# Attention start: tile 0's scores spread in three portions from two queues, tile 1's scores computed before the first head mix

## The chip, the cores and the metric

The kernel runs on one core of a Trainium2 chip. The metric is the device time of one execution in microseconds (us). Of the kernel before there are three runs: 768.92, 771.27 and 774.01 us (median 771.27). One further execution was profiled, and every row below is from it. PE is the matrix engine, DVE the vector engine, ACT the scalar engine, POOL the GpSimd engine, and SP the engine whose queue issues most DMAs.

## What is computed

Attention whose heads are mixed twice, and then two gated or squared feed-forward layers, all in float32. The part that matters is the start of the attention:

```python
scores = scale * np.matmul(q, k.transpose(0, 1, 3, 2))        # 2 batches, 12 heads, 448 x 448
scores = np.einsum('bhij,hg->bgij', scores, w_pre)            # mix of the heads
scores = scores - np.max(scores, axis=-1, keepdims=True)
attn = np.exp(scores)
attn = attn / (np.sum(attn, axis=-1, keepdims=True) + 1e-09)
attn = np.einsum('bhij,hg->bgij', attn, w_post)               # second mix
return np.matmul(attn, v)
```

The feed-forward layers follow: `x = (x @ w_a) * (x @ w_b) @ w_out`, then `relu(x @ w_in) ** 2 @ w_out`.

## The kernel before

The 448 query rows of a batch are cut into four tiles (120, 120, 120 and 88 rows), so that there are eight tiles over the two batches. A tile goes through these steps:

- `load_q` (L119) fetches the tile's queries, `load_k` (L124) one pair of heads' keys.
- `qk(b, t, c)` (L133) computes the scores of heads 2c and 2c+1: two matmuls into two PSUM banks, queries on the partitions. The trace records a float32 matmul as two rows, so one `qk` is "x4".
- `qk_out` (L145) copies each head's scores from PSUM to SBUF (even heads on ACT at L153, odd heads on DVE at L151) and issues the DMA that spreads them into the buffer `G[t % 2]` (L157). After it, partition 13 k + h of G holds head h of ten query rows, and G's second index r counts twelve such groups of ten rows. One DMA per head moves all twelve groups, 210 KB; head 11 needs a second small one of one partition (L160), so a tile has 13 of them, all on SP's queue.
- `premix` (L167) is the first mix: one matmul per group r, which reads G[:, r, :] of all heads. Two groups make a pair m; tile 0 has the pairs 0 to 5. One `premix` call is two matmuls ("x4"). Its PSUM tag T has three banks.
- `smin`, `sexp`, `weights2` (softmax), `post` (L209, second mix), `evac` (L231), `av` (L247) follow pair by pair.

The order on each engine is the order in which the code is written. The main loop runs over the pairs n: `premix` of pair n+1, `qk_out` of what is pending, `post` of pair n, the softmax of pair n+1, then the work that a table `mid` sets for slot n. For the tile after tile 0 the table places `qk` c at slot (c * 3) // 6, so the slots 0, 1 and 2 hold two `qk` each for tile 1. The slots 3 to 8 hold one `qk` each for tile 2. `load_q` of tile 2 stands at slot 0.

Ahead of the loop: SP loads six `ks` (keys) and then the queries of tile 1; POOL's queue loads tile 0's queries, `wpre_sb` and `wp`, and then POOL clears G[0] while DVE clears G[1] (L274, L275). PE runs nine dummy matmuls (`busy(9)`, L282), tile 0's six `qk`, and eighteen dummy matmuls (`busy(18)`). SP issues tile 0's 13 spreads, then the load of `v` (1344 KB) and the queries of tile 2.

Of the kernel before, what the change touches and what calls it, by code (L numbers as in the profile page):

```python
# [7 lines left out]
F32 = mybir.dt.float32  # L8
# [7 lines left out]
B, H, S, D = 2, 12, 448, 64  # L16
# [31 lines left out]
def half_rows(t, r):  # L48
    return KG if (r + 1) * ROW <= ROWS[t] else (ROWS[t] - r * ROW) // 2
# [3 lines left out]
def place(k, h):  # L53
    return 64 if (k, h) == (ROW - 1, H - 1) else PK * k + h
# [3 lines left out]
def attention_moe_kernel(  # L58
# [10 lines left out]
    nc = tc.nc  # L69
# [7 lines left out]
    def ps(tag):  # L77
        return psum.tile([128, 512], F32, tag=tag, name=tag, bufs=PB[tag])
# [5 lines left out]
    wpre_sb = const.tile([128, 128], F32, name="wpre_sb")  # L84
# [5 lines left out]
    def xpair(b, i, dtype):  # L90
        return outer.tile([128, 2, S], dtype, tag=f"x{b}_{i}", name=f"x{b}_{i}")
# [9 lines left out]
    s_p = att.enter_context(tc.tile_pool(name="s", bufs=4))  # L101
    e_p = att.enter_context(tc.tile_pool(name="e", bufs=2))
    a_p = att.enter_context(tc.tile_pool(name="a", bufs=2))

    G = [sb.tile([128, H, S], F32, name=f"G{i}") for i in range(2)]
    A = {}
# [6 lines left out]
    Sps = []  # L113
# [2 lines left out]
    vv = {}  # L116
    AVp = {}

    def load_q(b, t, eng=nc.sync):  # L119
        x = w_p.tile([128, UW], F32, tag="wc", name="q", bufs=2)  # L120
        eng.dma_start(out=x[:, 0:6 * TILE], in_=qT[b, t])
        qq[b, t] = x

    def load_k(b, c, eng=nc.sync):  # L124
        kk[b, c] = single(f"ks{6 * b + c}", F32)
        eng.dma_start(out=kk[b, c], in_=kT[b, c])

    def load_v(b, eng=nc.sync):
        x = sb.tile([JP, NJ, DM], F32, tag="v", name="v")
        eng.dma_start(out=x, in_=v[b])  # L130
        vv[b] = x


    def qk(b, t, c, tags=("qk", "qk")):
        n = ROWS[t]
        p = [ps(tag) for tag in tags]
        for e in range(2):
            o = 64 * e
            nc.tensor.matmul(  # L139
                p[e][0:n, 0:S], qq[b, t][o:o + 64, c * TILE:c * TILE + n], kk[b, c][o:o + 64, :], start=True, stop=True  # L140
            )
        for e in range(2):
            Sps.append((b, t, 2 * c + e, p[e]))

    def qk_out(stage=None):  # L145
        while Sps:
            b, t, h, p = Sps.pop(0)
            n = ROWS[t]
            s = stage[h // 2][0:TILE, h % 2, :] if stage else s_p.tile([TILE, S], F32, tag="s", name="s")
            if h % 2:  # L150
                nc.vector.tensor_copy(s[0:n], p[0:n, 0:S])  # L151
            else:
                nc.scalar.copy(s[0:n], p[0:n, 0:S])  # L153
            g = G[t % 2]
            full = n // ROW
            last = ROW - 1 if h == H - 1 else ROW
            nc.sync.dma_start(out=g[h:PK * (last - 1) + h + 1:PK, 0:full, :], in_=s[0:last * full])  # L157
            if last < ROW:
                o = place(last, h)
                nc.sync.dma_start(out=g[o:o + 1, 0:full, :], in_=s[last * full:ROW * full])  # L160
            rem = (n - full * ROW) // 2
            for f in range(2 if rem else 0):
                o = full * ROW + f * rem
                a = place(f * KG, h)
                nc.sync.dma_start(out=g[a:a + PK * (rem - 1) + 1:PK, full, :], in_=s[o:o + rem])

    def premix(b, m):  # L167
        t, r, n = PAIRS[m]
# [56 lines left out]
    def evac(b, m, f):  # L225
        t, r, n = PAIRS[m]
        if r == 0 and f == 0:
            A[b, t] = a_p.tile([JP, NJ * H, TILE], F32, tag="a", name="a")
        a = A[b, t]
        p = Pps[b, m][f]  # L230
        k = half_rows(t, r + n - 1)  # L231
        src = p[0:JP, 0:n * NJ * H * KG].rearrange("p (n g k) -> p n g k", n=n, k=KG)[:, :, :, 0:k]
        o = r * ROW + f * k
        dst = a[:, :, o:o + (n - 1) * ROW + k]
        if n == 2:
            dst = a[:, :, r * ROW:(r + 2) * ROW].rearrange("p g (n i) -> p n g i", n=2)[:, :, :, f * KG:f * KG + KG]
        else:
            src = src[:, 0]
        if f:
            nc.vector.tensor_copy(dst, src)  # L240
        else:
            nc.scalar.copy(dst, src)
# [23 lines left out]

    warm = const.tile([128, 1], F16, name="warm")
    nc.vector.memset(warm, 0.0)
    load_q(0, 0, nc.gpsimd)
    for c in range(NC):  # L270
        load_k(0, c)
    nc.gpsimd.dma_start(out=wpre_sb, in_=wpre)
    nc.gpsimd.dma_start(out=wp, in_=wpost)
    nc.gpsimd.memset(G[0], 0.0)  # L274
    nc.vector.memset(G[1], 0.0)  # L275
    nc.vector.tensor_scalar(wpre_sb, wpre_sb, -0.125, None, ALU.mult)


    def busy(n):
        p = ps("av")  # L280
        for _ in range(n):
            nc.tensor.matmul(p[0:1, 0:S], warm, warm.to_broadcast([128, S]), start=True, stop=True)  # L282

    busy(9)
    load_q(0, 1)
    stage0 = [xpair(b, i, F32) for b in range(B) for i in range(NC // 2)]
    tags0 = (("qk", "qk"), ("T", "T"), ("post", "post"))
    for c in range(NC):
        qk(0, 0, c, tags0[c % 3])
# [10 lines left out]
    act_l, dve_l, mid = {}, {}, {}  # L300

    def at(d, slot, *f):
        d.setdefault(max(slot, 0), []).append(f)

    for ti, (b, t) in enumerate(tiles):
        s0, sp = base[ti], span[ti]
        if ti + 1 < len(tiles):
            nxt = tiles[ti + 1]
            for c in range(NC):
                at(mid, s0 - 3 + c if ti else (c * (sp - 3)) // NC, qk, *nxt, c)  # L310
            if ti + 2 < len(tiles):
                at(mid, s0 - 2, load_q, *tiles[ti + 2])
            if nxt[1] == NTL - 1 and nxt[0] + 1 < B:
                for c in range(NC):
                    at(mid, s0 + c // 2, load_k, nxt[0] + 1, c)
        if ti > 0:
            pb, pt = tiles[ti - 1]
            for c in range(NC):
                s = s0 + 1 + (c * (sp - 1)) // NC
                at(mid, s, av, pb, pt, c)  # L320
                if c % 2:
                    at(mid, s, av_out, pb, pt, c // 2)
            if pt == NTL - 1 and pb + 1 < B:
                at(mid, s0 + sp, load_v, pb + 1)
# [80 lines left out]
    s0 = base[-1]  # L405
    s1 = base[-2]
# [189 lines left out]
def _layout(i):  # L596
    import numpy as np

    f = np.float32
    q, k, v = i["q"], i["k"], i["v"]  # L600
    qT = np.zeros((B, NTL, 128, NC, TILE), f)
    for t in range(NTL):
        n = ROWS[t]
        full = n // ROW
        p = np.arange(full * ROW)
        col = np.concatenate([ROW * (p % full) + p // full, np.arange(full * ROW, n)]) + OFFS[t]
        x = q[:, :, col, :].reshape(B, NC, 2, n, D).transpose(0, 2, 4, 1, 3)
        qT[:, t, :, :, 0:n] = x.reshape(B, 128, NC, n)
    kT = k.reshape(B, NC, 2, S, D).transpose(0, 1, 2, 4, 3).reshape(B, NC, 128, S)
    vl = v.reshape(B, H, NJ, JP, D).transpose(0, 3, 2, 1, 4).reshape(B, JP, NJ, DM)  # L610
    wpre = np.zeros((128, 128), f)
    wpost = np.zeros((128, H, KG), f)
    for n in range(ROW):
        o = [place(n, h) for h in range(H)]
        wpre[np.ix_(o, o)] = i["w_pre"]
        wpost[o, :, n % KG] = i["w_post"]

    def units(m):
        kk, n = m.shape
        x = m.reshape(kk // 128, 128, n // 128, 128).transpose(2, 0, 1, 3)  # L620
        return x.reshape(-1, US, 128, 128).transpose(0, 2, 1, 3).reshape(-1, 128, US * 128)

    ua, ub = units(i["moe_w_a"]), units(i["moe_w_b"])
    ab = np.stack([ua, ub], 1).reshape(-1, 128, US * 128)
    wall = np.concatenate([ab, units(i["moe_w_out"]), units(i["moe2_w_in"]), units(i["moe2_w_out"])], 0).view(np.uint64)
    return {"qT": qT.reshape(B, NTL, 128, NC * TILE), "kT": kT, "v": vl, "wpre": wpre, "wpost": wpost, "w": wall}
# [20 lines left out]
```

## Time and profile before

| what | value |
|---|---|
| runs | 768.92, 771.27, 774.01 us |
| the profiled execution | 769.89 us |
| its span (first to last instruction) | 768.1 us |
| PE busy | 745.7 us, 97% of the span |
| DVE, ACT, POOL busy | 63%, 40%, 2% |
| SP's queue and the like (hardware queue), share of 16 DMA engines | 33.2% |

The span is 1.8 us shorter than the execution's own time. The chain of waits that ended last is PE for 95% of the span. The page cuts the span into 40 slices of 19.2 us: PE's row begins 6, 7 and is 8 or 9 in tenths from the third slice on, and PE's granted clock is 9, 7 and then 9 in tenths.

### The profile page before, as it was taken

The numbers are of one execution on the slowest core, as the hardware profiler recorded it, in microseconds if no ns is written. First come the engines' busy times: TensorE is split into PE (matmuls) and PEld (weight loads), VectorE is DVE, ScalarE is ACT, GpSimd is POOL, SyncE is SP. The second block draws the span as 40 slices with busy tenths as digits, with TensorE's granted clock in tenths as the row PEclk, the third lists the DMA queues.
The fourth block names the chain that finished last, engine by engine and source line by source line (L and its number), as shares of the span: only waits on it lengthen the run. The fifth ranks groups of instructions, "written<-read, shape, count | busy, mean of one in ns | idle before, by whom it ended". The sixth has DMA issues, their size and how long they took to land.

```text
span 768.1 us, 12411 instructions
## 1 busy us (share of the span) xinstructions
PE 745.7 (97%) x5055; PEld 617.8 (80%) x5055; DVE 487.4 (63%) x817; ACT 309.1 (40%) x559; POOL 18.0 (2%) x16
## 2 busy tenths in 40 slices
PE   6799999998999999999999999999999999999998
PEld 2356666665667799999999999999999999999997
DVE  4366656565667767676667666556888888654540
ACT  2355554454456443334333323223555554322220
POOL 3000000000002300000000000000000000000000
PEclk9799999999999999999999999999999999999999
DMA  6543243426141113323323323323233332434310
GB/s 215 170 132 102 82 129 116 120 74 188 57 146 58 61 65 125 123 83 123 124 83 124 123 83 124 124 82 124 83 123 101 106 124 88 160 129 134 126 48 36
DMA packets 26696, 84.85 MB, mean 110 GB/s; under 512 B 2896, under 2 KB 16736, under 8 KB 26416
## 3 DMA queue, kind: packets, MB, share of 16 engines
q1 hardware_dynamic: 26496, 83.59, 33.2%
q8 instruction: 40, 0.66, 0.4%
q0 software_dynamic: 144, 0.47, 0.2%
q14 instruction: 16, 0.13, 0.0%
HBM read 62.03 MB, written 2.75 MB: 84 GB/s over the span
## 4 chain that ended last, share of the span: by engine, by line
PE 95%; DMA 2%; SPq 1%; DVE 1%; ACT 0%; issue 0%; ACTq 0%; POOLq 0%
PE T L171 10%; PE post L219 10%; PE T L448 8%; PE T L449 8%; PE T L450 8%; PE qk L448 5%; PE post L449 5%; PE post L448 5%; PE post L450 5%; PE qk L449 5%; PE qk L450 5%; PE av L254 5%; PE qk L139 5%; PE av L450 3%; PE av L449 3%; PE av L448 3%
## 5 line engine op out<-in xcount | busy, mean ns | idle before, releaser
L372 ACT CAST wh<-wc 128x768 fp32r<-128x768 f32 x68 | 56.8, 835 | 122.3 <-DVE wc L366 108.8
L219 PEld LDWEIGHTS post<-w,e 64*112 64x112 f32 x1440 | 74.4, 174 | 29.8 <-PE T L171 21.5
L377 DVE TENSOR_TENSOR wl<-wc,wh 128x768 fp32r<-128x768 f32 x66 | 63.0, 955 | 48.1 <-ACT wh L372 48.1
L187 ACT ACTIVATE e<-T,nb 128x448 f32<-128x448 f32 x90 | 56.9, 633 | 88.0 <-DVE nb L179 87.9
L171 PE MATMUL T<-G,wpre_sb 128*128 128x448 f32 x180 | 82.3, 581 | 8.4 <-DMA G<-x 8.4
L449 PE MATMUL T<-m,wh 128*128 128x448 f32 x237 | 86.6, 365 | 0.0
L448 PE MATMUL T<-m,wh 128*128 128x448 f32 x237 | 86.6, 365 | 0.0
L450 PE MATMUL T<-m,wl 128*128 128x448 f32 x237 | 86.5, 365 | 0.0
L219 PE MATMUL post<-w,e 64*112 64x60 f32 x1440 | 80.5, 261 | 0.1
L179 DVE TENSOR_REDUCE nb<-T 128x1 f32<-128x448 f32 x90 | 55.8, 623 | 28.3 <-PE T L171 23.4
L171 PEld LDWEIGHTS T<-G,wpre_sb 128*128 128x128 f32 x180 | 31.6, 195 | 47.4 <-issue 46.1
L355 DVE SCALAR_TENSOR_TENSOR wa<-wr,wa 128x768 uint32<-128x768 uint32 x68 | 65.2, 959 | 2.3
L366 DVE SCALAR_TENSOR_TENSOR wc<-wc,wa 128x768 uint32<-128x768 uint32 x68 | 65.2, 958 | 2.3
L240 DVE COPY a<-post 112x480 f32<-112x480 f32 (+1 forms) x46 | 30.9, 671 | 49.6 <-PE post L219 49.6
L350 ACT ACTIVATE wc<-wr 128x768 f32<-128x768 f32 x68 | 61.4, 903 | 0.0
L254 PE MATMUL av<-a,v 112*64 112x120 f32 (+1 forms) x768 | 45.2, 264 | 5.2 <-DMA v<-v 3.0
L254 PEld LDWEIGHTS av<-a,v 112*64 112x64 f32 x768 | 37.0, 136 | 15.7 <-PE post L219 4.0
L362 DVE TENSOR_SCALAR wc<-wc 128x768 f32<-128x768 f32 x68 | 38.7, 569 | 16.3 <-ACT wc L350 16.3
L139 PE MATMUL qk<-ks,q 64*120 64x448 f32 (+1 forms) x176 | 44.9, 568 | 4.1 <-DMA q<-qT 2.3
L448 PEld LDWEIGHTS T<-m,wh 128*128 128x128 f32 x237 | 44.5, 188 | 3.5
L449 PEld LDWEIGHTS T<-m,wh 128*128 128x128 f32 x237 | 44.5, 188 | 3.5
L450 PEld LDWEIGHTS T<-m,wl 128*128 128x128 f32 x237 | 44.5, 188 | 3.5
(146 smaller groups left out, 1353.2 us busy)
## 6 DMA issues: line engine op xcount, KB each, us to landing
wr<-w SPq DMA_DIRECT2D x68, 768.0 KB
G<-s SPq DMA_DIRECT2D x55, 210.0 KB
G<-s SPq DMA_DIRECT2D x22, 140.0 KB
ks<-kT SPq DMA_DIRECT2D x12, 224.0 KB
v<-v SPq DMA_DIRECT2D x2, 1344.0 KB
outT<-ta SPq DMA_DIRECT2D x12, 224.0 KB
q<-qT SPq DMA_DIRECT2D x7, 360.0 KB
G<-x SPq DMA_DIRECT2D x11, 210.0 KB
```

The source lines that it names most:

```text
L139: nc.tensor.matmul(p[e][0:n, 0:S], qq[b, t][o:o + 64, c * TILE:c * TILE + n], kk[b, c][o:o + 64, :], start=True, stop=True)
L171: nc.tensor.matmul(p[0:GP, 0:S], wpre_sb[0:GP, 0:GP], G[t % 2][0:GP, r + i, :], start=True, stop=True)
L187: nc.scalar.activation(out=e[0:GP], in_=Tps.pop((b, m, i))[0:GP, 0:S], func=ACTF.Exp, bias=NB[b, m][0:GP, i:i + 1], scale=-1.0, accum_out= ...
L219: nc.tensor.matmul(p[f][0:JP, c:c + k], e[o:o + 64, j * JP:(j + 1) * JP], w2[o:o + 64, i, :], start=True, stop=True,)
L254: nc.tensor.matmul(p[64 * e:64 * e + 64, o:o + n], vv[b][:, j, g * D:(g + 1) * D], A[b, t][:, j * H + g, 0:n], start=(j == 0), stop=(j == ...
L350: nc.scalar.activation(out=st["c"], in_=rd(st["high"]), func=ACTF.Abs, scale=HSC)
L355: nc.vector.scalar_tensor_tensor(out=a, in0=st["high"], scalar=0x80000000, in1=a, op0=ALU.bitwise_and, op1=ALU.bitwise_or)
L366: nc.vector.scalar_tensor_tensor(out=cu, in0=cu, scalar=3, in1=st["a"], op0=ALU.logical_shift_left, op1=ALU.bitwise_or)
L377: eng.tensor_tensor(out=lo, in0=st["c"], in1=rd(st["hi"]), op=ALU.subtract)
L448: nc.tensor.matmul(p[:, 0:S], hi[:, sl], x[0], start=first, stop=False)
L449: nc.tensor.matmul(p[:, 0:S], hi[:, sl], x[1], start=False, stop=False)
L450: nc.tensor.matmul(p[:, 0:S], lo[:, sl], x[0], start=False, stop=last)
```

## The change

Tile 0's scores are spread in three portions of groups: 0 to 1, 2 to 5 and 6 to 11 (`GS`). The first portion's DMAs go out as each head is copied, even heads from SP, odd heads from POOL; the second and third portions are issued by SP, head by head, after that. Groups 0 to 1 are pair 0, groups 2 to 5 the pairs 1 and 2, groups 6 to 11 the pairs 3 to 5. The queries' rows are laid out on the host so that each portion's rows lie together. Tile 1's six `qk` move ahead of the loop, into a staging tile `s1` that takes one of the two buffers of pool `a`, and its 13 spreads are issued by POOL, after POOL has cleared G[1]. Tile 0's queries are loaded in three pieces from ACT's queue, ahead of ACT's table load, and `wpre_sb` behind them. G[0] is cleared in three pieces, by POOL, DVE and POOL. Eighteen dummy matmuls become four.

```diff
+GS = (0, 2, 6, 12)
...
-    def load_q(b, t, eng=nc.sync):
+    def load_q(b, t, engs=(nc.sync,)):
         x = w_p.tile([128, UW], F32, tag="wc", name="q", bufs=2)
-        eng.dma_start(out=x[:, 0:6 * TILE], in_=qT[b, t])
+        n = NC * TILE // len(engs)
+        for i, eng in enumerate(engs):
+            eng.dma_start(out=x[:, i * n:(i + 1) * n], in_=qT[b, t, :, i * n:(i + 1) * n])
         qq[b, t] = x
...
+    def qk_copy(t, h, p, s):
+        n = ROWS[t]
+        if h % 2:
+            nc.vector.tensor_copy(s[0:n], p[0:n, 0:S])
+        else:
+            nc.scalar.copy(s[0:n], p[0:n, 0:S])
+
+
+    def spread(t, h, s, r0, r1, eng=nc.sync):
+        g = G[t % 2]
+        n = r1 - r0
+        o = r0 * ROW
+        last = ROW - 1 if h == H - 1 else ROW
+        eng.dma_start(out=g[h:PK * (last - 1) + h + 1:PK, r0:r1, :], in_=s[o:o + last * n])
+        if last < ROW:
+            a = place(last, h)
+            eng.dma_start(out=g[a:a + 1, r0:r1, :], in_=s[o + last * n:o + ROW * n])
...
-            A[b, t] = a_p.tile([JP, NJ * H, TILE], F32, tag="a", name="a")
+            A[b, t] = a_p.tile([128, NJ * H, TILE], F32, tag="a", name="a")[0:JP]
...
-    load_q(0, 0, nc.gpsimd)
-    for c in range(NC):
+    for c in range(2):
         load_k(0, c)
-    nc.gpsimd.dma_start(out=wpre_sb, in_=wpre)
+    load_q(0, 0, (nc.scalar, nc.scalar, nc.scalar))
+    for c in range(2, NC):
+        load_k(0, c)
+    nc.scalar.dma_start(out=wpre_sb, in_=wpre)
     nc.gpsimd.dma_start(out=wp, in_=wpost)
-    nc.gpsimd.memset(G[0], 0.0)
-    nc.vector.memset(G[1], 0.0)
+    for i in range(3):
+        (nc.gpsimd, nc.vector)[i % 2].memset(G[0][:, GS[i]:GS[i + 1], :], 0.0)
     nc.vector.tensor_scalar(wpre_sb, wpre_sb, -0.125, None, ALU.mult)
...
     for c in range(NC):
         qk(0, 0, c, tags0[c % 3])
-        qk_out(stage0)
+        while Sps:
+            _, t, h, p = Sps.pop(0)
+            qk_copy(t, h, p, stage0[h])
+            spread(0, h, stage0[h], GS[0], GS[1], (nc.sync, nc.gpsimd)[h % 2])
+    nc.gpsimd.memset(G[1], 0.0)
+    for i in range(1, 3):
+        for h in range(H):
+            spread(0, h, stage0[h], GS[i], GS[i + 1])
+    s1 = a_p.tile([128, NJ * H, TILE], F32, tag="a", name="s1").rearrange("p g i -> p (g i)")
+    stage1 = [s1[0:TILE, h * S:(h + 1) * S] for h in range(H)]
+    for c in range(NC):
+        qk(0, 1, c, tags0[c % 3])
+        while Sps:
+            _, t, h, p = Sps.pop(0)
+            qk_copy(t, h, p, stage1[h])
+    for h in range(H):
+        spread(1, h, stage1[h], 0, ROWS[1] // ROW, nc.gpsimd)
     load_v(0)
-    busy(18)
+    busy(4)
...
-            for c in range(NC):
-                at(mid, s0 - 3 + c if ti else (c * (sp - 3)) // NC, qk, *nxt, c)
+            for c in range(NC if ti else 0):
+                at(mid, s0 - 3 + c, qk, *nxt, c)
```

On SP's queue the spreads of tile 0 read so before; each row is one DMA (or "x2" two alike), `x` is the staged scores of tile 0 by pairs of heads, G_83 is G[0].

```order
L157 DMA G_83<-x_0_118 10x12x448 x2
L157 DMA G_83<-x_1_119 10x12x448 x2
L157 DMA G_83<-x_2_120 10x12x448 x2
L157 DMA G_83<-x_0_121 10x12x448 x2
L157 DMA G_83<-x_1_122 10x12x448 x2
L157 DMA G_83<-x_2_123 10x12x448
L157 DMA G_83<-x_2_123 9x12x448
L160 DMA G_83<-x_2_123 1x12x448
L130 DMA v<-v 112x3072
L121 DMA q<-qT 128x720
```

Now the second portion ends and the third one runs as follows; six spreads of two groups and ten more of four stand ahead of these rows.

```order
L162 DMA G_83<-x_2_126 10x4x448
L162 DMA G_83<-x_2_126 9x4x448
L165 DMA G_83<-x_2_126 1x4x448
L162 DMA G_83<-x_0_121 10x6x448 x2
L162 DMA G_83<-x_1_122 10x6x448 x2
L162 DMA G_83<-x_2_123 10x6x448 x2
L162 DMA G_83<-x_0_124 10x6x448 x2
L162 DMA G_83<-x_1_125 10x6x448 x2
L162 DMA G_83<-x_2_126 10x6x448
L162 DMA G_83<-x_2_126 9x6x448
L165 DMA G_83<-x_2_126 1x6x448
L134 DMA v<-v 112x3072
```

Thirteen spreads have become 6 of two groups, 13 of four and 13 of six, 32 in all, and `v` and tile 2's queries stand behind all of them.

On PE the loop's first slots read so before; T is the first mix, post the second.

```order
L171 MATMUL T<-G_83,wpre_sb 128x448 x4
L219 MATMUL post<-w_206,e 112x60 x16
L139 MATMUL qk<-ks_89,q 120x448 x2
L139 MATMUL qk<-ks_91,q 120x448 x2
L171 MATMUL T<-G_83,wpre_sb 128x448 x2
L219 MATMUL post<-w_243,e 112x60 x16
L139 MATMUL qk<-ks_93,q 120x448 x2
L139 MATMUL qk<-ks_95,q 120x448 x2
```

Now the same slots, up to pair 5's first mix in the last row (the T rows are pairs 0 and 1, then 2, 3, 4 and 5):

```order
L185 MATMUL T<-G_83,wpre_sb 128x448 x4
L233 MATMUL post<-w_272,e 112x60 x16
L185 MATMUL T<-G_83,wpre_sb 128x448 x2
L233 MATMUL post<-w_309,e 112x60 x16
L185 MATMUL T<-G_83,wpre_sb 128x448 x2
L233 MATMUL post<-w_347,e 112x60 x16
L185 MATMUL T<-G_83,wpre_sb 128x448 x2
L233 MATMUL post<-w_383,e 112x60 x16
L143 MATMUL qk<-ks_87,q 120x448 x2
L185 MATMUL T<-G_83,wpre_sb 128x448 x2
```

The six `qk` of tile 1 have left the slots 0 to 2; tile 2's first `qk` stays ahead of pair 5.

POOL's queue held three loads and one clear at the start before. Now it reads as follows, from its second clear on (G_84 is G[1], s_203 the staging tile of tile 1):

```order
L291 MEMSET G_83 128x2688
L162 DMA G_83<-x_0_121 10x2x448
L162 DMA G_83<-x_1_122 10x2x448
L162 DMA G_83<-x_2_123 10x2x448
L162 DMA G_83<-x_0_124 10x2x448
L162 DMA G_83<-x_1_125 10x2x448
L162 DMA G_83<-x_2_126 9x2x448
L165 DMA G_83<-x_2_126 1x2x448
L311 MEMSET G_84 128x5376
L162 DMA G_84<-s_203 10x12x448 x11
L162 DMA G_84<-s_203 9x12x448
L165 DMA G_84<-s_203 1x12x448
```

The odd heads' part of the first portion, the clear of G[1] and the 13 spreads of tile 1 stand behind each other on it.

## Rows read from the trace of the kernel before

**Rows 1.** Chain of waits: start us, us, what; the stretch 12 to 30 us
```profile
12.90 0.76 SPq L157
...
16.32 1.10 SPq L157
...
19.20 3.83 DMA G<-x
23.03 0.41 issue
23.44 5.89 PE T L171 x8
```

**Rows 2.** Chain of waits, the loop's first slots
```profile
31.05 0.85 PE qk L139 x4
...
32.47 1.50 PE qk L139 x4
...
40.31 1.70 PE T L171 x4
...
50.87 1.70 PE T L171 x4
52.57 1.71 PE post L219 x32
54.28 0.81 PE qk L139 x4
55.09 1.70 PE T L171 x4
```

**Rows 3.** Timeline of SP's queue: start us, us, line, out<-in, xcount
```profile
8.39 10.75 SPq L157 DMA_DIRECT2D G<-x  x12
...
20.02 1.05 SPq L130 DMA_DIRECT2D v<-v  x1
...
80.62 0.77 SPq L157 DMA_DIRECT2D G<-s  x1
81.48 1.31 SPq L165 DMA_DIRECT2D G<-s  x2
```

**Rows 4.** Timeline of all engines, the first 8 us: [idle before <-releaser]
```profile
0.93 3.52 PE L282 MATMUL av<-warm 128*1 128x448 f16 x9 [0.93 <-DVE warm L268]
1.25 0.69 POOL L121 DMA_DIRECT2D q<-qT  x1 [0.81 <-POOLq L636]
...
1.96 4.54 DVE L275 MEMSET G<- 128x5376 f32 x1 [1.09 <-issue]
...
2.47 0.54 POOL L273 DMA_DIRECT2D wp<-wpost  x1
...
3.00 4.60 POOL L274 MEMSET G<- 128x5376 f32 x1
...
6.73 1.02 PE L139 MATMUL qk<-ks,q 64*120 64x448 f32 x4 [2.28 <-DMA q<-qT]
7.08 0.60 DVE L276 TENSOR_SCALAR wpre_sb<-wpre_sb 128x128 f32<-128x128 f32 x1 [0.58 <-DMA wpre_sb<-wpre]
```

**Rows 5.** Stretches: A:B length, busy (count) of each engine, granted clock, DMA share, GB/s
```profile
12.00:20.00 8.00, 3.03 (x16) 1.17 (x14) 0.20 (x1) 0.06 (x1) 0.00 (x0) 0.91 0.63 219
18.60:28.70 10.10, 5.26 (x7) 2.52 (x8) 1.66 (x5) 1.45 (x4) 0.00 (x0) 0.50 0.80 250
6.50:8.50 2.00, 1.77 (x10) 1.02 (x12) 1.23 (x2) 0.53 (x1) 1.09 (x1) 1.00 1.00 384
...
29.00:30.00 1.00, 1.00 (x16) 0.74 (x16) 0.99 (x2) 0.52 (x1) 0.00 (x0) 1.00 0.00 0
```

**Rows 6.** DMA issues of the first 30 us: queue, KB each, median us to landing
```profile
q<-qT POOLq DMA_DIRECT2D x1, 360.0 KB, 5.4
...
wp<-wpost POOLq DMA_DIRECT2D x1, 30.0 KB, 5.0
```

**Rows 7.** Stretch from 28.8 us to the end, same columns as the stretches above
```profile
28.80:768.00 739.20, 728.54 (x4998) 610.69 (x4996) 476.64 (x804) 303.13 (x548) 11.49 (x8) 1.00 0.32 106
```

More of the change, by code (lines that the diff above doesn't have):

```diff
@@ L143, in qk, with qk_out @@
             Sps.append((b, t, 2 * c + e, p[e]))
-    def qk_out(stage=None):
+    def qk_copy(t, h, p, s):
[13 more added lines that the diff above has]
+            eng.dma_start(out=g[a:a + 1, r0:r1, :], in_=s[o + last * n:o + ROW * n])
+    def qk_out():
         while Sps:
@@ L148, in qk_out @@
             n = ROWS[t]
[L149 to L154, printed above, removed]
-            full = n // ROW
[L156 to L160, printed above, removed]
+            s = s_p.tile([TILE, S], F32, tag="s", name="s")
+            qk_copy(t, h, p, s)
+            full = n // ROW
+            spread(t, h, s, 0, full)
             rem = (n - full * ROW) // 2
@@ L164, in qk_out @@
                 a = place(f * KG, h)
-                nc.sync.dma_start(out=g[a:a + PK * (rem - 1) + 1:PK, full, :], in_=s[o:o + rem])
+                nc.sync.dma_start(out=G[t % 2][a:a + PK * (rem - 1) + 1:PK, full, :], in_=s[o:o + rem])
     def premix(b, m):
@@ L285, in attention_moe_kernel @@
     load_q(0, 1)
-    stage0 = [xpair(b, i, F32) for b in range(B) for i in range(NC // 2)]
+    stages = [xpair(b, i, F32) for b in range(B) for i in range(NC // 2)]
+    stage0 = [x[0:TILE, e, :] for x in stages for e in range(2)]
     tags0 = (("qk", "qk"), ("T", "T"), ("post", "post"))
@@ L601, in _layout @@
     qT = np.zeros((B, NTL, 128, NC, TILE), f)
-    for t in range(NTL):
+    for b, t in np.ndindex(B, NTL):
         n = ROWS[t]
         full = n // ROW
[L605 to L608, printed above, removed]
+        col = []
+        g = GS if b + t == 0 else (0, full)
+        for r0, r1 in zip(g, g[1:]):
+            p = np.arange((r1 - r0) * ROW)
+            col.append(ROW * (r0 + p % (r1 - r0)) + p // (r1 - r0))
+        col = np.concatenate(col + [np.arange(full * ROW, n)]) + OFFS[t]
+        qT[b, t, :, :, 0:n] = q[b][:, col, :].reshape(NC, 2, n, D).transpose(1, 3, 0, 2).reshape(128, NC, n)
     kT = k.reshape(B, NC, 2, S, D).transpose(0, 1, 2, 4, 3).reshape(B, NC, 128, S)
```

## Prediction

> **What bounds the kernel now.** I read the stretches first. From 28.8 us to the end PE is busy for 728.5 of 739.2 us at full clock [rows 7]. So what the change can win lies ahead of that, and what it wins there goes through to the end nearly whole, because PE runs the same list of instructions afterwards. Next came the chain of waits at the start. There the reader is to see a chain of DMA issues, not of arithmetic: SP's queue issues tile 0's 13 spreads one behind the other, and the last one, issued at 19.20, lands 3.83 us later; PE begins the first mix 0.41 us after that, at 23.44 [rows 1]. The first two pairs of that mix take 5.89 us, since PE has idled from 15.03 to 23.44 by then (3.03 us of work in 12 to 20) and the granted clock is 0.50 of full, 1.2 GHz, until about 28.7 [rows 1, 5]. Third, the chain in the loop's first slots: slots 0 to 2 hold two `qk` each and last 40.31 - 33.97 = 6.34 us; the second `qk` waits for a PSUM bank, so that it takes 1.50 us instead of 0.81. From pair 4 on a slot is 1.70 + 1.71 + 0.81 = 4.22 us [rows 2]. (33.97 is the sum of 32.47 and 1.50.) Pair 5's first mix starts at 50.87, tile 1's at 55.09.
>
> **The yardstick.** From pair 5's first mix on, both programs hold the same PE rows. I therefore compute when it starts now, and take the difference to 50.87 off the profiled execution's 769.89 us (span 768.1 and 1.8 around it). The median of the three runs is 1.4 us above that execution; one per cent, about what a measurement of this kernel can tell from no change, is 7.7 us.
>
> **An earlier start.** Before, the first `qk` waited 2.28 us for the queries, which POOL's queue had issued at 1.25 and landed in 5.4 us [rows 4, 6]. Now three pieces on ACT's queue go out from the program's start. No row shows an ACT issue. At best the pieces are there when the dummy matmuls end, 0.93 + 3.52 = 4.45; at worst they take POOL's 5.4 us from about 0.8, and `qk` starts at 6.2. I take 4.5, because POOL's issue began only at 1.25 and moved all 360 KB, where the first `qk` needs one piece of 120 KB. SP's first spread came 8.39 - 6.73 = 1.66 us after the first `qk` [rows 3, 4]; so now at 6.2 (6.1 to 7.9).
>
> **32 issues instead of 13.** A spread costs SP 0.76 us, and the next starts 0.86 after it, but for a single long one of 1.10 [rows 1]. What decides is whether a spread of two to six groups costs less than one of twelve. A spread of eight groups cost 0.77, the same; a tiny one of fewer dimensions about 0.65 (1.31 for two) [rows 3]. The new ones have the dimensions of the 0.76 row, so I take 0.86 from start to start, and keep 0.71 (0.61 to 0.65 and the gap of 0.1) as the lower end. One long one adds 0.34. The last issue of portion 2 (the 19th) then starts at 6.2 + 18 x 0.86 = 21.7, the last of portion 3 (the 32nd) at 6.2 + 31 x 0.86 + 0.34 = 33.2.
>
> **Landing.** The 3.83 us came behind a backlog: SP issued 215 KB per 0.86 us, 250 GB/s, and 219 GB/s moved [rows 5]; 31 GB/s over 8 us is 0.25 MB, 1.1 us at that rate. The new spreads ask for 125 GB/s at most, so I take 2.8 us (bounds: 0.76, the issue itself, and 3.83). The Trainium skill, DMA: Bandwidth & Descriptors, section Anatomy of one DMA, fits about 2.0 us and size over 436 GB/s for one DMA, 2.25 for 105 KB; by it the sum would be 0.55 lower, 762.5. The trace's 3.83 for 21 KB is higher, and no run here shows a spread on a quiet queue.
>
> **The loop now.** Portion 2 lets pair 1's mix start at 21.7 + 2.8 + 0.4 = 24.9, after another long wait and so at 1.2 GHz: 5.89 / 2 = 2.95. `post` of pair 0 takes at most twice 1.71, then pair 2's mix 1.70 and `post` of pair 1 1.71: PE is through at 34.7 at the latest. Portion 3 lets pair 3's mix start at 33.2 + 2.8 + 0.4 = 36.4, so SP's queue decides, with 1.7 us to spare. From there two slots without `qk` and one `qk`: 2 x (1.70 + 1.71) + 0.81 = 7.63 [rows 2], pair 5's mix at 44.0. That is 6.9 us earlier: **763.0 us** (769.89 - 6.9).
>
> **What lies under cover.** Tile 1's six `qk`, their copies and the four dummy matmuls stand in PE's wait, between about 9 and 24.9; without that cover they would cost 6 x 0.81 = 4.9. Pair 0's mix needs the first portion, also POOL's part of it. POOL takes 0.54 to 0.69 per issue and 5.0 to 5.4 to land [rows 4, 6]: with DVE's first copy behind `wpre_sb` at about 7, the seven are out at 12 and landed at 17, 8 us before pair 1 needs PE. POOL then clears G[1] in 4.6 [rows 4], issues 13 spreads and has them landed near 30; tile 1's first mix needs them at 48.2. `v` and tile 2's queries go out from 34.1 instead of 20.02; before, both had moved by 29 (0 GB/s in 29 to 30) [rows 3, 5], 9 us later, backlog included. So the queries are there at 43.1 at the latest and `qk` of slot 3 needs them at 43.2: hidden, but only just.
>
> **The rivals.**
> - *The third portion lands later or finds PE cold, smaller gain.* POOL's 13 spreads at 0.69 ask for 312 GB/s beside SP's 83 to 125; the most that a stretch moved is 384 [rows 5]. Short by 11 to 53 GB/s for 9 us, 0.1 to 0.5 MB, is 0.5 to 2.2 us if SP's part bears it all. Or PE loses its clock in the wait ahead of pair 3: two mixes at half clock cost 5.89 - 3.40 = 2.5. Against that: after 2.28 us of idling the first `qk` ran at full clock [rows 4, 5]. Either gives 763.5 to 765.5; I name 765.4.
> - *Small spreads issue faster.* At 0.71 the 32nd starts at 28.5, portion 3 is there at 31.7, and then pair 1's side decides: 6.2 + 18 x 0.71 + 3.2 + 2.95 + 3.42 + 1.70 + 1.71 = 32.0. Pair 5 at 39.6, 11.3 us earlier: 758.6. For it speaks the 0.65 row, against it the eight groups at 0.77 [rows 3].
> - *POOL's queue is late: slower.* POOL holds 7 issues, a clear and 13 issues in a row. With a us per issue, G[1] is complete at 7.0 + 7a + 4.6 + 12a + 5.4 = 17.0 + 19a. Up to a = 1.64 nothing shows (48.2); at 2.0 the gain is gone (55.1); from 2.4 on the kernel is slower by over 1%, and at 2.5 it takes 779.3. No row shows POOL issuing a spread; its loads cost 0.54 to 0.69, and the 0.54 one at 2.47 lay inside DVE's clear [rows 4]. The Trainium skill, SBUF — State Buffer, section SBUF: two separate sides, says that some DVE copies keep GpSimd from writing descriptors, and gives about 3.1 us for a DMA instead of 0.62; at a = 3.1 the result would be 790.7. DVE's copies here come out of PSUM, and no run here shows such a block.
> - *The portions are not told apart*, and pair 0 waits for all 32: its mix starts at 36.4 at half clock, then 5.89 + 1.71 + 3 x 3.41 + 0.81 puts pair 5 at 55.0, 4.2 us later: 774.1. The order of the rows alone does not exclude it, but the clears and reads are by groups.
>
> **How the numbers follow.** Forecast as summed (761 to 765): 0.58. Third portion late or cold: 0.18. Faster issue: 0.14. POOL late: 0.07 (0.04 of it from 2.4 on). Not told apart: 0.03. The limit of 1% is 762.2; the forecast's own spread, from the start (up to 1.7 later) and the landing (2.0 less to 1.0 more), lies under it for 0.22 of its 0.58. So faster 0.14 + 0.22 = 0.36, slower 0.04, within 1% the remaining 0.60. The range takes in the forecast, most of the later cases and the faster issue down to 758: 758.0 to 768.0.
>
> **What would show it.** In the profile after: SP's spreads of tile 0 begin near 6.2 and end near 33, 0.86 apart; PE waits on G three times, the first mix starts near 17, pair 1's near 25 and at half clock, pair 3's near 36.4, pair 5's near 44; slots 0 to 2 last 3.4 us where no wait stands in them; POOL's issues of spreads last under 1 us. The prediction is wrong if spreads cost by their groups, if POOL's issues last over 1.6 us, if pair 3's mix runs at half clock, or if `qk` of slot 3 waits for tile 2's queries.

## The result, and the profile after

The changed kernel takes 776.54 us (median of 13 runs, 774.24 to 781.11) where the kernel before takes 771.03 (13 runs, 768.92 to 774.01): a ratio of 1.0081 with a 95% interval of 1.0058 to 1.0103. So it is slower by 5.5 us, within the 1% of 7.7 us, where 8.0 us faster than the median (6.9 off the profiled execution) was forecast. The time lies outside the range of 758 to 768. The profiled execution took 777.43 us, 7.54 more than that of before.

The chain of waits of the changed kernel (start us, us, what):

```profile
20.16 0.97 SPq L162
...
21.18 3.93 SPq L162
...
25.21 3.81 SPq L162
...
29.06 2.22 SPq L165
...
37.51 3.31 PE T L185 x4
40.81 3.18 PE post L233 x32
43.99 3.14 PE T L185 x4
47.13 1.72 PE post L233 x32
48.85 1.70 PE T L185 x4
...
56.49 1.70 PE T L185 x4
```

The reader should look at one kind of row: a DMA issue on SP's queue, which took 0.76 us in [rows 1], takes 3.93, 3.81 and 2.22 us here. These are the last three DMAs of portion 2 (L165 is head 11's single partition). Pair 1's mix, forecast for 24.9, starts at 37.51 and runs at half clock, and so do `post` of pair 0 and pair 2's mix. Pair 5's mix, the yardstick, starts at 56.49; before it was 50.87 [rows 2]. That is 5.62 us later. Most of the rest of the 7.54 comes where PE waits for `v` of the second batch (L268 is L254 of before; first the changed kernel, then the kernel before):

```profile
196.47 2.95 PE L268 MATMUL av<-a,v 112*64 112x120 f32 x32 [2.90 <-DMA v<-v]
```

```profile
190.96 1.86 PE L254 MATMUL av<-a,v 112*64 112x120 f32 x32 [3.02 <-DMA v<-v]
```

After the wait PE runs at half clock from 197.05 to 200.46 in the changed kernel; the `post` behind it starts at 201.58, where it started at 194.46 before, so 7.1 of the 7.54 us stand by then.

The timeline of PE (start us, us; in brackets the idle time before the row and what ended it) and that of POOL's queue:

```profile
4.37 1.76 PE L143 MATMUL qk<-ks,q 64*120 64x448 f32 x4
...
16.19 1.77 PE L185 MATMUL T<-G,wpre_sb 128*128 128x448 f32 x4
37.49 3.32 PE L185 MATMUL T<-G,wpre_sb 128*128 128x448 f32 x4 [19.53 <-DMA G<-x]
```

```profile
9.02 3.40 POOL L162 DMA_DIRECT2D G<-x  x6 [3.85 <-DVE x L152]
...
17.85 5.34 POOL L162 DMA_DIRECT2D G<-s  x9 [0.30 <-POOL G L311]
24.95 0.58 POOL L162 DMA_DIRECT2D G<-s  x1 [1.76 <-DMA G<-s]
28.70 1.18 POOL L162 DMA_DIRECT2D G<-s  x2 [3.17 <-DMA G<-s]
```

`G<-s` is tile 1. POOL pushes nine of its 210 KB spreads out in 5.34 us from 17.85 on, while SP still has six DMAs of portion 2 to issue. Who got the DMA engines is in the queues of the stretch 20 to 34 us (packets, MB, share of 16 engines; q0 is POOL's queue, q1 SP's):

```profile
DMA packets 1034, 2.55 MB, mean 182 GB/s; under 512 B 441, under 2 KB 621, under 8 KB 1034
...
q0 software_dynamic: 811, 2.22, 71.9%
q1 hardware_dynamic: 223, 0.32, 11.8%
...
G<-s POOLq DMA_DIRECT2D x8, 210.0 KB, 12.2
```

SP, whose data PE waits for, moved 0.32 of 2.55 MB, and the total was 182 GB/s, less than the 219 that SP moved alone before [rows 5]. The packet records behind these rows give sizes and mean durations:

```
stretch                  queue   data packets
before, 12 to 20 us      SP      976 of 1792 B,  82 ns each
after,  20 to 34 us      SP      180 of 1792 B, 144 ns each
after,  20 to 34 us      POOL    413 of 5376 B, 380 ns each
```

A POOL packet has the bytes of three rows of 1792 B and lasts 380 ns, nearly five times the 82 ns of an SP packet before. That SP's packets stand behind POOL's long ones is what these rows suggest; they don't show the order on a DMA engine.

### The profile page after: what moved, and what is told of

It reads as the page before. It is cut to its first block, busy times and chain, and to the rows that moved or that the text cites. A ratio compares the mean times of both kernels' runs of the same rounds, so it can differ in the third digit from the quotient of the medians.

```text
span 775.6 us, 12437 instructions
## 1 busy us (share of the span) xinstructions
PE 745.4 (96%) x5041; PEld 619.1 (80%) x5041; DVE 483.6 (62%) x817; ACT 309.0 (40%) x559; POOL 31.6 (4%) x36
## 4 chain that ended last, share of the span: by engine, by line
PE 93%; DMA 2%; SPq 2%; POOL 1%; DVE 1%; issue 0%; ACTq 0%; ACT 0%; POOLq 0%
PE T L185 10%; PE post L233 10%; PE T L481 8%; PE T L483 8%; PE T L482 8%; PE av L268 5%; PE qk L481 5%; PE post L481 5%; PE qk L483 5%; PE post L482 5%; PE qk L482 5%; PE post L483 5%; PE qk L143 4%; PE av L482 3%; PE av L483 3%; PE av L481 3%
## 5 line engine op out<-in xcount | busy, mean ns | idle before, releaser
L193 DVE TENSOR_REDUCE nb<-T 128x1 f32<-128x448 f32 x90 | 55.6, 623 | 36.2 <-PE T L185 31.5
L254 DVE COPY a<-post 112x480 f32<-112x480 f32 (+1 forms) x46 | 30.8, 670 | 51.0 <-PE post L233 51.0
L268 PE MATMUL av<-a,v 112*64 112x120 f32 (+1 forms) x768 | 46.3, 268 | 5.1 <-DMA v<-v 2.9
L268 PEld LDWEIGHTS av<-a,v 112*64 112x64 f32 x768 | 37.9, 139 | 15.6 <-PE post L233 4.0
L143 PE MATMUL qk<-ks,q 64*120 64x448 f32 (+1 forms) x160 | 40.1, 576 | 0.6 <-DVE x L152 0.6
```

Of the source, the lines that this page charges most:

```text
L143: nc.tensor.matmul(p[e][0:n, 0:S], qq[b, t][o:o + 64, c * TILE:c * TILE + n], kk[b, c][o:o + 64, :], start=True, stop=True)
L268: nc.tensor.matmul(p[64 * e:64 * e + 64, o:o + n], vv[b][:, j, g * D:(g + 1) * D], A[b, t][:, j * H + g, 0:n], start=(j == 0), stop=(j == ...
```

## The experiments

Theory A: POOL's spreads of tile 1 (`G<-s`) take the DMA engines from SP's portion 2; that is the loss. Theory B: 32 issues in three portions are themselves what is slow on SP. Theory C, in some expectations: tile 1's 2.6 MB cost the same from whichever queue. All edits are to the changed kernel.

**e1, without tile 1's spreads.**

```diff
-    for h in range(H):
-        spread(1, h, stage1[h], 0, ROWS[1] // ROW, nc.gpsimd)
```

> The changed kernel without tile 1's 13 spreads from POOL's queue: G[1] stays zero for tile 1, so tile 1's part of the attention is left out; all other instructions stay. Theory A (POOL's spreads take the DMA engines from SP's small ones, and SP's issues stall behind that): SP's spreads of tile 0 run 0.86 us apart to the end near 34, pair 1's first mix starts near 25 instead of 37.5, pair 3's near 36.5, pair 5's near 44 instead of 56.4; the time is 762 to 765. Theory B (the 32 small spreads choke themselves, whatever POOL does): SP's issues of 2 to 4 us stay, pair 1's mix stays after 33, the time stays at 773 to 777. Theory C (the bytes of tile 1's spread, from whichever queue) expects the same as A here.

Measured: 766.27 us, ratio 0.9917 (0.9899 to 0.9935). SP's queue, and PE (timelines):

```profile
6.79 15.53 SPq L162 DMA_DIRECT2D G<-x  x18
22.38 0.64 SPq L165 DMA_DIRECT2D G<-x  x1
23.12 9.56 SPq L162 DMA_DIRECT2D G<-x  x12
32.72 0.71 SPq L165 DMA_DIRECT2D G<-x  x1
```

```profile
24.59 3.33 PE L185 MATMUL T<-G,wpre_sb 128*128 128x448 f32 x4 [6.67 <-DMA G<-x]
...
35.52 1.77 PE L185 MATMUL T<-G,wpre_sb 128*128 128x448 f32 x4
...
42.53 1.02 PE L143 MATMUL qk<-ks,q 64*120 64x448 f32 x4
43.47 1.77 PE L185 MATMUL T<-G,wpre_sb 128*128 128x448 f32 x4
```

The mixes of pairs 1, 3 and 5 start at 24.59, 35.52 and 43.47; the prediction had 24.9, 36.4 and 44.0. Its times for tile 0 hold within 0.9 us as long as POOL's 13 spreads are not there. Those 13 cost 12.9 us at pair 1 (37.49 - 24.59). The time is still 1.3 us over the expected 765: the profiled execution took 765.86, 4.0 us less than that of before, though pair 5 came 7.3 us earlier. Behind the wait for the second batch's `v` PE ran at half clock from 183.43 to 190.26, so that the `av` and the mix there took 3.47 and 3.23 us, where they took 1.86 and 1.77 before; that is 3.1 us of the difference.

**e2, the 13 spreads from ACT's queue.**

```diff
-        spread(1, h, stage1[h], 0, ROWS[1] // ROW, nc.gpsimd)
+        spread(1, h, stage1[h], 0, ROWS[1] // ROW, nc.scalar)
```

> Tile 1's 13 spreads at the same place, but issued from ACT's queue instead of POOL's. Theory A with POOL's queue as the cause (its packets are larger and get more of an engine's time): SP's issues stay below about 1.2 us, pair 1's mix starts before 28, though pair 0's softmax stands behind ACT's 13 issues (about 11 us, to 27); the time is 763 to 768. Theory C (any 2.6 MB at that time): SP's issues stretch to 2 to 4 us as in the changed kernel, pair 1's mix starts after 33, the time is 773 to 777.

Measured: 783.70 us, ratio 1.0149 (1.0117 to 1.0180), where 763 to 768 us was expected: a miss. On SP it came near to what theory A has: no issue over 1.90 us (about 1.2 was expected), and pair 1's first group mixed at 26.64 (before 28). The queues of 20 to 34 us (q10 is ACT's), ACT, the chain of waits, and PE:

```profile
DMA packets 1508, 2.39 MB, mean 171 GB/s; under 512 B 174, under 2 KB 1508, under 8 KB 1508
...
q10 hardware_dynamic: 864, 1.43, 31.5%
q1 hardware_dynamic: 644, 0.96, 26.5%
```

```profile
17.41 23.05 ACTq L162 DMA_DIRECT2D G<-s  x12
```

```profile
17.41 1.45 ACTq L162
...
18.96 5.62 DMA G<-s
...
24.65 3.99 DMA G<-s
...
28.66 5.76 DMA G<-x
...
34.49 4.84 DMA G<-s
```

```profile
42.12 1.86 PE L185 MATMUL T<-G,wpre_sb 128*128 128x448 f32 x2 [13.65 <-ACT e L201]
```

With tile 1's spreads in packets all under 2 KB, SP gets 0.96 MB instead of 0.32. That is not the packets alone: ACT moved 1.43 MB in this stretch where POOL moved 2.22, and by 23.2 us it had issued three spreads where POOL had issued nine. The issuing engine pays: the twelve spreads hold ACT for 23.05 us, and the exponentials of pair 0 stand behind them, so PE waits 13.65 us for ACT. A single issue took 0.79 us in the median and 1.45 at most; the rest of the 23.05 ACT waits between its issues for earlier transfers to land, by the chain for its own and once for one of SP's. I had left out that what stands behind such a wait on an engine that also computes waits too.

**e3, the 13 spreads later.** Three further clears of the same buffer push them behind portion 2.

```diff
-    nc.gpsimd.memset(G[1], 0.0)
+    for _ in range(4):
+        nc.gpsimd.memset(G[1], 0.0)
```

> POOL clears G[1] four times instead of once, so that its 13 spreads start about 13.8 us later, near 31.7, when SP has nearly issued all of tile 0's. Theory A: portion 2 lands undisturbed, pair 1's mix near 25; pair 3's near 37 to 39, since the last few spreads of portion 3 meet POOL's; G[1] is complete between 43 and 50, needed near 48; the time is 763 to 768. Theory B: SP's issues stall as before at 20 to 35, the time 773 to 777.

Measured: 775.33 us, ratio 1.0055 (1.0036 to 1.0075), where 763 to 768 us was expected: a miss. POOL's spreads now begin at 31.93; SP's issues are undisturbed (last one 33.19), pair 1's mix starts at 24.79. PE further on:

```profile
41.38 3.33 PE L185 MATMUL T<-G,wpre_sb 128*128 128x448 f32 x4 [7.28 <-DMA G<-x]
...
52.51 1.85 PE L143 MATMUL qk<-ks,q 64*120 64x448 f32 x4 [2.49 <-DMA q<-qT]
54.29 3.35 PE L185 MATMUL T<-G,wpre_sb 128*128 128x448 f32 x4
```

The wait has moved with POOL's spreads: portion 3's last transfers, in flight from 31.9 on, hold pair 3 until 41.38 (35.52 in e1), and then tile 2's queries are late. That portion 2 lands undisturbed is as A has it. The time is not: putting off the 13 spreads by 14 us buys little, for whatever is in flight beside them pays. (The profiled execution took 778.33 us, 3.0 over the run's median, so these waits may be longer than usual.)

**e4, the portions alone.** Tile 1's `qk` and spreads stand where they stood before.

```diff
-    for c in range(NC):
-        qk(0, 1, c, tags0[c % 3])
...
-    for h in range(H):
-        spread(1, h, stage1[h], 0, ROWS[1] // ROW, nc.gpsimd)
-    busy(4)
+    busy(18)
-            for c in range(NC if ti else 0):
-                at(mid, s0 - 3 + c, qk, *nxt, c)
+            for c in range(NC):
+                at(mid, s0 - 3 + c if ti else (c * (sp - 3)) // NC, qk, *nxt, c)
```

> The portions, their queues, the loads from ACT and the clears as in the changed kernel, but tile 1's qk and spreads as in the kernel before (two qk in each of the slots 0 to 2, spreads from SP after them, 18 dummy matmuls). Theory A: pair 1's mix near 25 as in the run without tile 1's spreads, slots 0 to 2 take 6.3 us or a little more again, so pair 3's mix is near 41 (40.3 before) and the time is 768 to 773. Theory B: SP's issues stall without any POOL spread of tile 1, pair 1's mix after 33, the time above 777.

Measured: 780.00 us, ratio 1.0095 (1.0074 to 1.0116), where 768 to 773 us was expected: a miss. SP's issues of tile 0 take 0.64 to 0.96 us again and pair 1's mix starts at 24.83, which speaks against B once more. The time is lost to a wait of its own:

```profile
43.36 0.53 ACT L154 COPY s<-qk 120x448 f32<-120x448 f32 x1 [6.13 <-DMA G<-s]
```

```profile
43.95 2.76 PE L143 MATMUL qk<-ks,q 64*120 64x448 f32 x4 [6.58 <-ACT s L154]
```

Tile 1's spreads now stand on SP's queue behind the 32 of tile 0 and the load of `v` (1344 KB, issued at 33.68). The staging buffers they read come free late, ACT's copy waits for one, and the `qk` behind it waits 6.58 us for the PSUM bank. So the move of tile 1's `qk` ahead of the loop is not an extra: without it the portions lose.

**e5, PE kept busy over the wait.**

```diff
     premix(*plist[0])
+    busy(95)
```

> The changed kernel with 95 dummy matmuls between pair 0's first mix and what follows, so that PE does not idle while SP's spreads stall. Theory A (late portion 2 first, and the half clock behind the 19.5 us of idling as a second price): pair 1's mix stays near 37.5 but takes 1.7 us instead of 3.3, post of pair 0 1.7 instead of 3.2, pair 2's mix 1.7 instead of 3.1; portion 3 then ends the next wait near 45; pair 5's mix near 53 instead of 56.4, the time 772 to 774. If the clock costs nothing, the time stays at 776 to 777.

Measured: 775.24 us, ratio 1.0036 (1.0018 to 1.0053). The issues on SP stall as in the changed kernel (up to 4.32 us), and pair 1's mix starts no earlier, but it runs at full clock:

```profile
38.28 1.74 PE L185 MATMUL T<-G,wpre_sb 128*128 128x448 f32 x4 [2.01 <-DMA G<-x]
...
54.18 1.77 PE L185 MATMUL T<-G,wpre_sb 128*128 128x448 f32 x4
```

Pair 5's mix is at 54.18 (near 53 was expected) where the timeline of the changed kernel has 56.42: 2.2 us of the loss are the low clock after the wait. The profiled executions differ by as much (775.26 to 777.43), the ratios by 3.5 us. The starved queue is the larger part.

**e6, half of the 13 spreads from SP.** Odd heads' go behind tile 0's on SP; POOL keeps six.

```diff
-        spread(1, h, stage1[h], 0, ROWS[1] // ROW, nc.gpsimd)
+        spread(1, h, stage1[h], 0, ROWS[1] // ROW, (nc.gpsimd, nc.sync)[h % 2])
```

> Half the dose: of tile 1's 13 spreads POOL issues the 6 of the even heads at the same place, SP the 7 others behind tile 0's 32. Theory A (SP's spreads stall for as long as POOL's traffic lasts): POOL's six, 1.29 MB, last about half as long as the 13 did, SP's issues of over 2 us are one or two instead of three, and pair 1's mix starts between 28 and 32 (24.6 with none, 37.5 with 13). If the stall is set by something else of POOL's (its clear, its first spreads), pair 1's mix stays near 37. Time 768 to 774.

Measured: 777.45 us, ratio 1.0081 (1.0061 to 1.0101), over the expected 768 to 774.

```profile
31.89 3.33 PE L185 MATMUL T<-G,wpre_sb 128*128 128x448 f32 x4 [13.04 <-DMA G<-x]
...
54.13 1.85 PE L143 MATMUL qk<-ks,q 64*120 64x448 f32 x4 [6.81 <-DMA q<-qT]
55.92 3.35 PE L185 MATMUL T<-G,wpre_sb 128*128 128x448 f32 x4
```

Pair 1 follows the dose, about a us per spread:

| tile 1's spreads on POOL beside portion 2 | SP's last issue of portion 2 | pair 1's mix |
|---|---|---|
| 0 (e1) | 22.38 | 24.59 |
| 6 (e6) | 27.44 | 31.89 |
| 13 (the change) | 29.06 | 37.49 |

The 5.6 us won there go again at tile 2's queries, which stand behind seven more spreads and `v` on SP (issued at 45.16, PE waits 6.81 us). Hence the same time as the change by another road.

**b2, tile 1's spreads all from SP, tile 2's queries from ACT.**

```diff
+    load_q(0, 2, (nc.scalar,))
-        spread(1, h, stage1[h], 0, ROWS[1] // ROW, nc.gpsimd)
+        spread(1, h, stage1[h], 0, ROWS[1] // ROW)
-            if ti + 2 < len(tiles):
+            if 0 < ti and ti + 2 < len(tiles):
```

> Tile 1's 13 spreads from SP behind tile 0's 32, tile 2's queries loaded early from ACT, v behind the spreads; POOL issues only its part of the first portion. Theory A: nothing meets tile 0's spreads, pair 1's mix near 24.6, pair 3's near 35.5, pair 5's near 43.2; tile 1's spreads are issued by 44 and landed by 47, just when tile 1's first mix wants them; the time is 763 to 766, as in the run without tile 1's spreads. Theory C (tile 1's bytes at any time): a new wait of several us ahead of tile 1, 768 or more.

Measured: 769.08 us, ratio 0.9968 (0.9946 to 0.9990). Expected was 763 to 766: a miss. Pair 1's mix 25.10; pair 3's 36.48 after a wait of 2.30 us and at half clock; pair 5's 45.73, 5.1 us earlier than before, of which the profiled execution (767.86) keeps 2.0. The wait is for portion 3, whose last issue on SP started at 34.01 and had landed by 36.1. Here the clock was full again from 29.69 on (33.24 in e1), so PE was through with `post` of pair 1 at 34.2, and SP's queue decided when pair 3 starts.

**b3, as b2, and portions 2 and 3 shared between SP and ACT** (`(nc.sync, nc.scalar)[h % 2]`), tile 1's copies all on DVE.

> As the run with tile 1's spreads from SP, but portions 2 and 3 divided: even heads from SP, odd heads from ACT, and tile 1's scores copied by DVE alone. Theory A (queues of SP and ACT share the DMA engines fairly, and the issue time is what binds): portion 2 lands near 20, portion 3 near 26, pair 1's mix 20 to 22 and pair 3's 28 to 31, the time 755 to 760. If ACT's issues slow SP's as POOL's did, pair 3's mix is after 34 and the time is 763 or more.

Measured: 767.13 us, ratio 0.9933 (0.9913 to 0.9952), where 755 to 760 us was expected: a miss. Pair 1's first group is mixed early, at 21.56, but the second waits 5.31 us for ACT, whose exponential stands behind ACT's issues as in e2. Pair 5's mix 46.82.

**b1, all spreads shared between SP and POOL.** DVE clears G[1], tile 2's queries come from ACT as in b2.

```diff
+    nc.vector.memset(G[1], 0.0)
-    nc.gpsimd.memset(G[1], 0.0)
-            spread(0, h, stage0[h], GS[i], GS[i + 1])
+            spread(0, h, stage0[h], GS[i], GS[i + 1], (nc.sync, nc.gpsimd)[h % 2])
-        spread(1, h, stage1[h], 0, ROWS[1] // ROW, nc.gpsimd)
+        spread(1, h, stage1[h], 0, ROWS[1] // ROW, (nc.sync, nc.gpsimd)[h % 2])
```

> All spreads of tile 0 and tile 1 divided between SP (even heads) and POOL (odd heads), G[1] cleared by DVE at the start, tile 2's queries loaded early from ACT. If what costs is only the size and time of POOL's traffic beside SP's (theory A), portion 2 meets POOL spreads of 72 KB and portion 3 of 108 KB: SP's issues stretch in portion 3, pair 1's mix near 19 to 22, pair 3's near 26 to 32, the time 754 to 764. If POOL's queue shuts out SP's whatever the size, pair 1's mix is after 25 and the time is 765 to 775.

Measured: 762.64 us, ratio 0.9878 (0.9842 to 0.9915): faster than both kernels and within the expected 754 to 764, though pairs 1 and 3 come later than its 19 to 22 and 26 to 32.

```profile
24.57 3.32 PE L185 MATMUL T<-G,wpre_sb 128*128 128x448 f32 x4 [5.96 <-DMA G<-x]
...
33.48 1.77 PE L185 MATMUL T<-G,wpre_sb 128*128 128x448 f32 x4
...
41.11 1.77 PE L185 MATMUL T<-G,wpre_sb 128*128 128x448 f32 x4
```

POOL's long packets now carry portion 2 itself, ahead of tile 1's on the same queue. Pair 1 comes no earlier than in e1 (24.57 against 24.59), though SP has half the issues: its last one of portion 2 starts at 16.57 and takes 2.28 us, and PE starts 8.0 us after that start. Together with ACT's load of the queries, SP and POOL moved 198 GB/s from 16 to 20 us and 197 from 20 to 24, no more than SP alone before (219): the queues share the engines' time here and don't add to it. That load (360 KB, issued at 15.51) and the first spreads of portion 3 move beside portion 2; what they cost it was not tested apart.

**b4, b1 with 28 dummy matmuls behind pair 0's mix.**

> The two-queue version with 28 dummy matmuls (5.2 us) between pair 0's first mix and what follows, so that PE does not idle ahead of pair 1's mix at 24.6. Theory A: pair 1's mix takes 1.7 us instead of 3.3 and post of pair 0 1.7 instead of about 2, pair 2's mix starts near 28 instead of 30.1; all else 2 us earlier: 759 to 762. If portion 3 then ends the wait (it lands near 27), less is won; without any gain 762 to 763.

Measured: 762.70 us, ratio 0.9889 (0.9865 to 0.9913), the same as b1. Pair 1's mix runs at full clock (24.93, 1.74 us), but pair 3's then waits 4.55 us for portion 3 and starts at 36.36, at half clock: PE has become early enough to meet tile 1's spreads on POOL. The profiled execution is the slowest of the six, 766.89 us, 4.2 over their median; how much of this wait the others have is not shown.

**b5 and b6, b1 and b4 with tile 1's spreads from SP alone**, behind tile 0's.

```diff
-        spread(1, h, stage1[h], 0, ROWS[1] // ROW, (nc.sync, nc.gpsimd)[h % 2])
+        spread(1, h, stage1[h], 0, ROWS[1] // ROW, nc.sync)
```

> Tile 0's three portions by SP (even heads) and POOL (odd heads), as in b1; tile 1's 13 spreads all from SP behind them, so that POOL has nothing queued beside portion 3. Theory A (POOL's packets starve SP's queue wherever both have much queued): portion 2 is as in b1, pair 1's mix at 24 to 25 at half clock; tile 1's spreads are issued by about 34 on SP; pair 5's mix stays near 41 to 42, as in b1, since the half clock and not portion 3 sets the order there; ratio 0.985 to 0.992. Theory B (SP's queue is slow by its own count of issues): SP's 32 issues reach 35 to 40 us, queries come early from ACT, nothing on PE's path moves either; then B differs only in SP's issues, 0.84 apart and without any over 1.3 us by A, spread out by B.

> b5 with 28 dummy matmuls behind pair 0's mix, which keep the clock full over the wait for portion 2 (in b4 they did, but portion 3 then waited 4.55 us, at SP issues of up to 2 us that stood beside POOL's spreads of tile 1). Theory A: without POOL's spreads of tile 1, portion 3 lands by about 33 and pair 3's mix starts at 32 to 33.5, pair 5's mix at 40 to 41, ratio 0.984 to 0.990. Theory B (the wait in b4 is the volume of tile 0's own second half, not POOL's tile 1): pair 3's mix stays at 35 to 36.5 and the ratio at 0.989, as in b4.

Measured: b5 762.26 us, ratio 0.9875 (0.9860 to 0.9891); b6 762.10 us, ratio 0.9878 (0.9858 to 0.9899). PE in b6:

```profile
25.09 1.74 PE L185 MATMUL T<-G,wpre_sb 128*128 128x448 f32 x4 [1.04 <-DMA G<-x]
...
31.89 1.77 PE L185 MATMUL T<-G,wpre_sb 128*128 128x448 f32 x4
...
39.53 1.77 PE L185 MATMUL T<-G,wpre_sb 128*128 128x448 f32 x4
```

Pair 3's wait of b4 is gone (31.89 after 36.36): in b4's profile it was POOL's tile 1, not tile 0's own second half. PE works without a wait from 25.09 to pair 5, whose mix comes at 39.53, 11.3 us before that of the kernel before. Two smaller expectations for b5 did not come: portion 2's issues on SP reached 2.21 us beside POOL's half of it, and tile 1's last issue on SP was at 37.20, not by 34. Between b1, b5 and b6 the runs show no difference (762.1 to 762.6 us). That b6 is 1.1 us ahead of b5 at pair 5 does not come out in the medians, whose intervals are wider than that.

## Why the prediction was wrong

- **The step that failed** is the term "POOL's 13 spreads ask for 312 GB/s beside SP's 83 to 125 ... 0.1 to 0.5 MB, 0.5 to 2.2 us". In the sum of 763.0 itself it stands at nothing; only a rival has it, at this price. The mechanism was named and the size was off by a factor of about six or more: 12.9 us at pair 1. Two inputs were wrong. First, the limit of 384 GB/s was read from a stretch of loads, at a DMA share of 1.00; the stretch of the spreads in the same group shows 219 GB/s at a share of 0.63 with a backlog behind it [rows 5]. That is near what spreads could move (233 in b6, from 28 to 37 us, with SP alone again). By it, POOL's 2.58 MB and the 0.36 MB that SP still had to issue at 17.85 take 13.4 us, to 31.3, and with 2.2 to land pair 1 would have started near 33.5: an estimate from these rows, but one that says "slower". At the 182 GB/s measured it gives 36.2, against 37.49. Second, I let both queues share by what they ask for; SP got 0.32 of 2.55 MB.
- **Where it hit** was wrong too: I put the price on portion 3. POOL's spreads began at 17.85, in portion 2, whose wait was not hidden by anything; a stall there goes through whole. The prediction's own times say so: POOL's seven issues out at 12 and a clear of 4.6 put its first spread of tile 1 near 16.6, before the last issue of portion 2 at 21.7. From pair 1's mix to pair 5's the profile has 18.98 us (37.51 to 56.49) and the forecast 19.1 (24.9 to 44.0). So the one term is the whole miss up to pair 5, 12.5 us: 7.4 us of it in SP's issues (the last of portion 2 at 29.06 for 21.7) and 5.2 in the landing (8.4 for 3.2).
- **The yardstick leaked too.** The forecast let what is won or lost at pair 5 go through to the end. Against before, the changed kernel loses another 1.9 us behind it, and e1 gives back 3.3 of its 7.3, mostly behind the wait for the second batch's `v`. So even without POOL's spreads the time is 766.27 and not 763.0.
- **The rival on the other side** had the right sign and a wrong mechanism. POOL's issues cost 0.55 to 0.64 us, as its loads did (0.54 to 0.69), and never came near its threshold of 2.0 to 2.4; SP was late, not POOL.
- **Right: the cost of an issue.** Spreads of two to six groups cost SP 0.75 us, not less than those of twelve, about 0.79 to 0.85 apart; "small spreads issue faster" is refuted.
- **Right: the portions are told apart.** Pair 0's mix ran at 16.19 (forecast 17), long before the last of portions 2 and 3 had been issued at 42.57.
- **Right: the start.** `qk` at 4.37 (4.5), and SP's first spread at 6.77 (6.2). The first `qk` took 1.76 us where it took 1.02 before, at a granted clock of 1.00 in the stretch 4.3 to 6.0 us; why stays open. The DMA issues on ACT, for which no row stood before, took 0.41 to 0.46 us.
- **Nearly right: the landing.** In e1, 2.21 us pass from the start of portion 2's last issue to PE's start; I took 2.8 + 0.4. The Trainium skill (DMA: Bandwidth & Descriptors, Anatomy of one DMA) has 2.0 us and size over 436 GB/s, a fit made on GpSimd's path; on SP's quiet queue it was nearer than my value from a backlogged one. Beside POOL's spreads, with 8.4 us, it is far off.
- **Right in the number, open in the binder: the last stretch.** The forecast had SP's queue decide, at 36.4, with 1.7 us to spare. In e1 PE reaches pair 3 at 35.52 without a wait, so PE decides, 0.9 us from the forecast, partly by luck: pair 2's mix took 2.86 us, most of it at half clock, where the forecast had 1.70. In b2, where the clock came back earlier, SP's queue decides, at 36.48. In e1 tile 2's queries landed 8.5 us after their issue at 34.03, and `qk` waited shortly for them: "hidden, but only just".

## What to carry to other kernels

Read the limit for a transfer from a stretch with the same kind of transfer, and look whether a backlog stands behind it: here 219 GB/s at 0.63 of the engines was near the ceiling, and 384 belonged to loads. Work that is moved into a wait is free on the idle compute engine, but not for the transfer that the wait is for: its DMAs belong behind that transfer on the same queue (b5, b6), or must be counted against it. And where DMA issues can block, or wait for earlier transfers to land, put them on a queue with no arithmetic behind it.

## What the runs showed of the hardware

- **Queues don't share by need.** POOL merges three rows of a spread into one packet of 5376 B (380 ns), SP and ACT send each row of 1792 B alone (82 to 144 ns). Beside POOL's spreads SP got 13% of the bytes, beside ACT's 40% (0.96 of 2.39 MB). Two things differ there: the packets, and how many spreads were out at a time (nine from POOL by 23.2 us, three from ACT). The Trainium skill (DMA: Bandwidth & Descriptors, Queues, rings and completion order) says that a DMA engine takes turns between queues, one whole packet at a time. The direction agrees. Even turns of the packets that the trace records would make the bytes 3 to 1, and it has 7 to 1, with 413 POOL packets to 180; whether a turn is one such record no run here shows. So packet size, which I did not vary by itself, is argued and not shown as the cause.
- **An issue can block, and a queue can wait for a landing.** When its transfers were slow, single issues of SP went from 0.75 to 3.93 us. ACT's in e2 stayed at 0.79 in the median, but between them ACT waited for earlier transfers to land; POOL did so after nine issues (1.76 and 3.17 us above). What stands behind on the same engine waits too.
- **The clock after similar waits.** PE idles 2.5 to 3.6 us for `v` of the second batch in the kernels named here. The granted clock then stayed full in the kernel before (3.02 us), in b1 (2.54) and in e6 (2.53), and fell to half in the changed kernel (2.90), e1 (3.27), b5 (3.59) and b6 (2.73). A fall made the 32 `av` matmuls take 2.95 us in the changed kernel and 3.47 in e1, b5 and b6, where the kernel before took 1.86. In b2 a wait of 2.30 us cost pair 3 its clock; the first `qk` of [rows 4] kept it after 2.28. From the length of such a wait alone I could not tell which it would be.
